# Decay attention with split operands: score operands stacked to 128 rows in batches 1 to 3

## The chip, the cores and the metric

The kernel runs on one core of one Trainium2 chip. The metric is the device time of one execution in microseconds (us); lower is better. TensorE (PE) multiplies, VectorE (DVE), ScalarE (ACT) and GpSimd (POOL) work on vectors, and SyncE's queue (SP) starts the transfers.

## What is computed

Attention with a decay and a causal mask (4 batches, 8 heads, 576 tokens, head width 64), then two dense layers. Cut to what matters:

```python
scores = scale * np.matmul(q, k.transpose(0, 1, 3, 2))
cum = np.cumsum(np.log(np.clip(f, 0.0001, 1.0)), axis=-1)
decay = cum[:, :, :, None] - cum[:, :, None, :]
scores = np.where(causal, -1e9, scores + decay)
scores = scores - np.max(scores, axis=-1, keepdims=True)
attn = np.exp(scores)
attn = attn / (np.sum(attn, axis=-1, keepdims=True) + 1e-09)
out = np.matmul(attn, v)
# then x = out as [2304, 512]
x = swish_1702(x @ w_in) @ w_out        # 512 -> 2048 -> 512
x = prelu(x @ w2_in, alpha) @ w2_out    # 512 -> 2048 -> 512
```

## The kernel before

**Order.** Nothing is issued where it is written. Each step is put into a plan (`plan.add`) with its costs on the engines that could do it, what it reads and writes, and a priority. `Plan.run` (L108) then places every step by these costs: it takes the step that can start first, attention before first-layer matmuls, and emits the instructions in that order. Each engine runs its own list in order. PE steps carry a mode: 0 for the full array, 1 for two 64-row halves, 2 for a split by columns; the planner counts 105 ns for a change of mode and avoids it for a while (L123 to L150). A tile belongs to a pool with a fixed number of slots, and a slot comes free when its last reader is done.

**Stages.** Attention works on a pair of heads at a time: batch 0 in two sweeps, then batches 1 to 3 with both chunks of a pair in turn, that is 12 pairs. Chunk 0 is queries 0 to 255, chunk 1 is queries 256 to 575. The first layer's matmuls (`gemm1`, L866) for blocks of 256 or 384 tokens are interleaved with the attention of later tokens and go on alone when it ends. Afterwards come the first layer's second half (L955), the second layer (L1045 and L1123) and the output. While batch 0 and the start of batch 1 run, DVE, ACT and POOL also turn the first layer's weights, which arrive as 64-bit numbers, into fp32 (L504 to L512).

**A pair of heads.** For precision an fp32 operand is split into a rounded part and the rest (KH and KL, QH and QL). Both heads share a tile: head 0 on partitions 0 to 63, head 1 on 64 to 127. In batches 1 to 3 `load_qk` (L531) fetches 32-row pieces, transposes them on DVE (L543), copies to the rounded part (L373 on ACT or L375 on DVE) and subtracts for the rest (L378 on DVE or POOL). DK holds the decay of the keys in two rows per head, and DQ the ones and the negated maxima of the queries.

- `chunk` finds the row maxima: QH times KH and ones times DK, each as one matmul per head on 64 rows, side by side (L669); the 64-row tail tile uses a zero-padded tile Z on the full array (L662, L663). DVE adds the mask and reduces (L678), POOL joins two halves of the tail (L687), PE turns the maxima (L695), and ACT or DVE writes them negated into DQ for both heads at once (L705, L707).
- `chunk2` computes the scores again, transposed, in four products (KH QH, KH QL, KL QH, DK DQ) for both heads side by side on 64 rows each (L794). ACT exponentiates into e (L801), POOL zeroes what is above the diagonal (L717).
- `after_scores` multiplies with the values. Chunk 0 uses fp32 products split by columns, 64 output columns per head part (L729, mode 2). Long tiles of chunk 1 are split into eh and el and multiplied on the full array (L758); the others go in fp32 (L735), the tail tile of 64 rows in mode 1. At last DVE transposes the sums (L815, L818), takes the reciprocal (L824), and multiplies (L835) into xr.

Pools that matter: KH, KL and DK have two slots, QH, QL and DQ three, e four.

Of the kernel before, what the change touches and what calls it, by code (L numbers as in the profile page):

```python
# [51 lines left out]
class Buf:  # L52
    def __init__(self, pool=None):
        self.pool = pool
        self.log = []
# [19 lines left out]
class Plan:  # L75
# [5 lines left out]
    def add(self, alts, fn, reads=(), writes=(), pri=0.0, lag=0.0, mode=0):  # L81
# [108 lines left out]
def kernel(  # L190
# [13 lines left out]
    nc = tc.nc  # L204
# [85 lines left out]
    p_z = sb("att", "Z", 2, [P, P], F32R)  # L290
# [16 lines left out]
    p_e = sb("att", "e", 4, [P, 2, 384])  # L307
# [5 lines left out]
    att_pools = [p_z, p_rk, p_rq, p_tk, p_tq, p_kh, p_kl, p_dk, p_qh, p_ql, p_dq, p_vr, p_vh, p_vl, p_mx, p_e, p_eh, p_el, p_tr, p_sm, p_rc]  # L313
# [68 lines left out]

    def a_out(n):
# [46 lines left out]
    for nm, p, view, n, val in (  # L430
        ("dk", p_dk, lambda x: (x.bitcast(F32), x[0:3].bitcast(F32), x[64:67].bitcast(F32)), 3 * S, (0.0, 1.0, 1.0)),
        ("z", p_z, lambda x: x.bitcast(F32), P, 0.0),
        ("dq", p_dq, lambda x: x.bitcast(F32), S - SPLIT, 0.0),
        ("mx", p_mx, lambda x: (x.bitcast(F32), x[:, 136:204].bitcast(F32), x[64:P, 138:139].bitcast(F32), x[0:64, 202:203].bitcast(F32)), 280, (-1.0, -0.5, 0.0, 0.0)),
        ("vr", p_vr, lambda x: x.rearrange("p t h c -> p t (h c)")[:, :, D:3 * D], NKT * P, 1.0),
# [10 lines left out]
    def filled(nm, p):  # L446
        return [fill[nm, len(p.bufs) - 1]] if len(p.bufs) <= p.n else []

# [82 lines left out]
    def load_qk(src, b, h0, c0, w, p_r, p_t, hi, lo, o0, pri, actq):  # L531

        raw, T = Buf(p_r), Buf(p_t)
# [10 lines left out]
        plan.add(a_copy(w), lambda e: copy(e, hi.ap[:, o0:o0 + w], T.ap[:, :w]), [T], [hi], pri)  # L544
        plan.add(a_sub(w), lambda e: sub(e, lo.ap[:, o0:o0 + w], T.ap[:, :w], hi.ap[:, o0:o0 + w].bitcast(F32)), [T, hi], [lo], pri)
# [24 lines left out]
    def prep_q(u, q0, q1, pri, actq, pet):  # L570
        b, h0, m = u["b"], 2 * u["hp"], q1 - q0
        qh, ql, dq = (Buf(x) for x in (p_qh, p_ql, p_dq))
        fdq = filled("dq", p_dq)
        if pet:
            load_pe(q, b, h0, q0, m, p_rq, qh, ql, 0, 0, pri)
        else:
            load_qk(q, b, h0, q0, m, p_rq, p_tq, qh, ql, 0, pri, actq)
        z = None
        if q0:
            z = Buf(p_z)  # L580
            fz = filled("z", p_z)
            for hh in range(2):
                plan.add(a_copy(64), lambda e, hh=hh: copy(
                    e, z.ap[64 * hh:64 * hh + 64, 64 * hh:64 * hh + 64], qh.ap[64 * hh:64 * hh + 64, m - 64:m].bitcast(F32)
                ), [qh, *fz], [(z, hh)], pri)
        return dict(u, z=z, fdq=fdq, qh=qh, ql=ql, dq=dq)

    def prep(b, hp, n, pri, early, actq, plain, pet):
        h0 = 2 * hp
        kh, kl, dk = (Buf(x) for x in (p_kh, p_kl, p_dk))  # L590
        fdk = filled("dk", p_dk)
        if pet:
            for i, (lo, hi) in enumerate(((0, SPLIT), (SPLIT, n))[:1 + (n > SPLIT)]):
# [581 lines left out]
```

## Time and profile before

| | us |
|---|---|
| three runs | 1023.01, 1023.96, 1024.02 |
| median | 1023.96 |
| profiled execution | 1022.32 |
| its span | 1020.6 |

The profile is of one execution. Times in it count from the start of the span. A row of the timeline gives a start, a length and an instruction; matmuls follow each other before the earlier has ended, so the distance from one start to the next says more than the length. In a matmul row `64*128 64x320` means 64 rows by 128 columns of fixed operand, and a moving operand of 64 rows by 320 columns; `x2` are two instructions merged.

### The profile page before, as it was taken

To read this page: it belongs to the slowest core of one execution; us is meant where nothing else is said; L and a number is where in the kernel's file an instruction comes from. 1 tells how busy PE (TensorE), PEld (TensorE's weight loads), DVE (VectorE), ACT (ScalarE), POOL (GpSimd) and SP (SyncE) were. 2 spreads that over 40 slices of the span, in tenths; PEclk is the share of its full clock that TensorE was granted. 3 is DMA by queue.
4 is the path that set the end of the run, shared out by engine and by line. 5 is a ranking of instruction groups with operands and counts; after the bars stand their busy time and mean duration, and the time that the engine had idled before them with its cause. 6 is when DMAs were issued, how large, how long until landed. Compare 5 with 4: busy or idle time off the path is not lost.

```text
span 1020.6 us, 17794 instructions
## 1 busy us (share of the span) xinstructions
PE 995.1 (98%) x6187; PEld 880.2 (86%) x6187; DVE 711.2 (70%) x1506; ACT 522.1 (51%) x1087; POOL 125.7 (12%) x209
## 2 busy tenths in 40 slices
PE   6799999999999999999999999999999999999997
PEld 4588789989888899988888988999999988888886
DVE  5688987767665493149996556567985866666773
ACT  4477755545444293258874554455774732222322
POOL 6124332323121100000000000000200110000000
PEclk9899999999999999999999999999999999999999
DMA  4597663443221176236765354655793534342451
GB/s 103 147 197 176 157 144 96 89 90 68 73 62 59 40 260 225 101 108 193 223 216 161 110 144 126 205 184 163 225 313 126 173 121 123 113 140 83 129 144 63
DMA packets 180089, 144.69 MB, mean 142 GB/s; under 512 B 101152, under 2 KB 155088, under 8 KB 180000
## 3 DMA queue, kind: packets, MB, share of 16 engines
q1 hardware_dynamic: 180000, 143.57, 48.3%
q8 instruction: 48, 0.79, 0.3%
q14 instruction: 41, 0.34, 0.1%
HBM read 96.14 MB, written 47.33 MB: 141 GB/s over the span
## 4 chain that ended last, share of the span: by engine, by line
PE 89%; DMA 4%; DVE 3%; issue 1%; ACT 1%; SPq 1%; POOL 0%; DVEq 0%; ACTq 0%; POOLq 0%
PE bk L866 20%; PE bk L955 19%; PE bk L1123 19%; PE bk L1045 13%; PE bk L794 5%; PE bk L758 3%; PE bk L669 2%; PE bk L735 2%; PE bk L729 2%; DMA rk<-in_k_dram 1%; DMA h2scr<-go 1%; DMA ba<-y1scr 1%; PE bk L695 1%; PE bk L564 1%; DMA wraw<-in_moe_w_out_dram 1%
## 5 line engine op out<-in xcount | busy, mean ns | idle before, releaser
L866 PE MATMUL bk<-xh,wA 128*128 128x384 f32 (+1 forms) x896 | 220.0, 319 | 1.5 <-POOL wA L378 1.3
L373 ACT CAST qh<-qg 128x512 fp32r<-128x512 f32 (+1 forms) x159 | 91.9, 579 | 170.8 <-DVE qg L921 117.0
L378 DVE TENSOR_TENSOR ql<-qg,qh 128x512 fp32r<-128x512 f32 (+1 forms) x158 | 100.7, 638 | 101.1 <-PE bk L955 50.6
L866 PEld LDWEIGHTS bk<-xh,wA 128*128 128x128 f32 x896 | 156.4, 189 | 12.3 <-issue 5.8
L1123 PE MATMUL bk<-wS,qh 128*128 128x512 f32 x576 | 145.7, 389 | 0.0
L866 PE MATMUL bk<-xl,wA 128*128 128x384 f32 (+1 forms) x448 | 140.0, 312 | 0.0
L1123 PEld LDWEIGHTS bk<-wS,qh 128*128 128x128 f32 x576 | 108.1, 188 | 22.4
L1045 PE MATMUL bk<-xsb,wS 128*128 128x384 f32 x576 | 108.1, 335 | 3.9 <-DVE go L1067 3.9
L678 DVE CUSTOM_DVE_ANT_0 bk<-bk,mask 128x512 f32<-128x512 f32 (+4 forms) x160 | 75.4, 494 | 45.0 <-PE bk L669 28.9
L1045 PEld LDWEIGHTS bk<-xsb,wS 128*128 128x128 f32 x576 | 100.3, 188 | 5.5 <-DVE go L1067 5.2
L955 PE MATMUL bk<-qh,woa 128*128 128x512 f32 (+1 forms) x440 | 99.5, 368 | 0.0
L373 ACT COPY gg<-bk 128x384 f32<-128x384 f32 (+1 forms) x109 | 47.4, 435 | 93.8 <-PE bk L866 86.0
L955 PEld LDWEIGHTS bk<-qh,woa 128*128 128x128 f32 x440 | 77.3, 189 | 14.0 <-ACT qh L373 0.4
L866 PEld LDWEIGHTS bk<-xl,wA 128*128 128x128 f32 x448 | 84.6, 189 | 0.1
L1045 PE MATMUL bk<-xsa,wS 128*128 128x384 f32 x432 | 82.6, 335 | 0.0
L801 ACT ACTIVATE e<-bk 128x384 f32<-128x384 f32 (+3 forms) x192 | 60.3, 396 | 40.7 <-PE bk L794 40.6
L1123 PE MATMUL bk<-wS,ql 128*128 128x512 f32 x288 | 80.4, 389 | 0.0
L1045 PEld LDWEIGHTS bk<-xsa,wS 128*128 128x128 f32 x432 | 75.6, 188 | 0.4 <-DVE xsa L378 0.3
L914 DVE SCALAR_TENSOR_TENSOR qg<-qg,qr 128x512 f32<-128x512 f32 (+1 forms) x80 | 50.8, 636 | 23.6 <-ACT qg L913 23.2
L1123 PEld LDWEIGHTS bk<-wS,ql 128*128 128x128 f32 x288 | 54.1, 188 | 11.2
L913 ACT ACTIVATE qg<-qr 128x512 f32<-128x512 f32 (+1 forms) x80 | 47.0, 588 | 22.5 <-DVE ql L378 20.9
L955 PE MATMUL bk<-ql,woa 128*128 128x512 f32 (+1 forms) x220 | 54.1, 368 | 0.0
(163 smaller groups left out, 1775.7 us busy)
## 6 DMA issues: line engine op xcount, KB each, us to landing
h2scr<-go SPq DMA_DIRECT2D x96, 192.0 KB
wraw<-in_moe_w_in_dram SPq DMA_DIRECT2D x32, 512.0 KB
wraw<-in_moe_w_out_dram SPq DMA_DIRECT2D x32, 512.0 KB
qr<-h1scr SPq DMA_DIRECT2D x64, 256.0 KB
qr<-h2scr SPq DMA_DIRECT2D x64, 256.0 KB
h1scr<-gg SPq DMA_DIRECT2D x64, 192.0 KB
ba<-y1scr SPq DMA_DIRECT2D x24, 384.0 KB
h1scr<-gg SPq DMA_DIRECT2D x48, 128.0 KB
```

What stands on the lines that cost most here:

```text
L373: nc.scalar.copy(dst, src)
L378: E[e].tensor_tensor(dst, a, b, op=ALU.subtract)
L678: plan.add([("DVE", c_dve(c1 - c0) + 90.0)], lambda e, pm=pm, c0=c0, c1=c1, mk=mk, m0=m0, col=col, f0=f0: nc.vector.tensor_tensor_reduce(p ...
L758: nc.tensor.matmul(pb[hh].ap[:l.shape[1], s0 - q0:n], l, rhs.ap[:w, hh, :m], start=st, stop=sp, skip_group_check=True,)
L794: nc.tensor.matmul(pss[hh].ap[:w, o_:o_ + m], x.ap[r, a:a + w], y.ap[r, s0 - q0:n], start=i == 0, stop=i == 3, skip_group_check=True)
L801: plan.add([("ACT", c_act(x1 - x0, True))], lambda e, hh=hh, pss=pss, e32=e32, w=w, x0=x0, x1=x1: nc.scalar.activation(e32.ap[:w, hh, :x1 ...
L866: nc.tensor.matmul(ph.ap[:, :n], w.ap[:, a, c, :], x[c // 2].ap[:, c % 2, :n], start=(c == 0 and j == 0), stop=(c == KT - 1 and j == 2))
L913: plan.add([("ACT", c_act(n))], lambda e: nc.scalar.activation(g.ap[:, :n], raw.ap[:, :n], AF.Tanh, scale=0.851), [raw], [g], pri)
L914: plan.add([("DVE", c_dve(n), 0.0, True)], lambda e: nc.vector.scalar_tensor_tensor(g.ap[:, :n], g.ap[:, :n], 1.0, raw.ap[:, :n], op0=ALU. ...
L955: nc.tensor.matmul(py[d].ap[:, :n], w[:, a, d * P:(d + 1) * P], (lo if x else h).ap[:, :n], start=(k == 0 and (a, x) == (0, 0)), stop=(k = ...
L1045: nc.tensor.matmul(out.ap[:, :XH], w[:, a, t, c, :], x.ap[:, b, c, :], start=(st and c == 0 and i == 0), stop=(c == 1 and i == 2), skip_gr ...
L1123: nc.tensor.matmul(py[t].ap, (lo if x else h).ap[:, t * P:(t + 1) * P], w[:, a], start=(k == 0 and (a, x) == (0, 0)), stop=(k == NM - 1 an ...
```

## The change

In batches 1 to 3 each head gets a plane of its own with 128 rows. KA holds a head's rounded keys in 64 rows, and beside them the decay rows; KB holds the rest of the keys in 64 rows and the rounded keys in the other 64. QA and QB are laid out to match: against KB stands the rounded query beside the rest, so that one product over 128 rows gives KL QH and KH QL together, and KA QA gives KH QH and the decay term (66 rows for the maxima and 67 for the scores of head 0, 128 of head 1). So a score tile has two products per head instead of four, and a maxima tile one instead of two, all in mode 0. To fill the planes, `load_qk` copies and subtracts by half (one half for each head) and moves the rounded halves across with a second copy (`a_move`, on ACT, DVE or POOL). The ones and zeros are set by POOL memsets at a slot's first use (`refill`), and one row of QA for each chunk. The negated maxima are evicted head by head. Chunk 0 of these batches takes the full-width fp32 value product (L735) and the by-head normalisation that chunk 1 has. The fp32 product of the 64-row tail tile takes 128 rows with zeros in all batches. The separate tq tile goes, tk serves both, the query planes have two slots, and e three. Batch 0 keeps its products in views of the new tiles.

The diff, cut to its core:

```diff
...
-    p_tq = sb("att", "tq", 1, [P, S - SPLIT])
-
-    p_kh = sb("att", "KH", 2, [P, S], F32R)
-    p_kl = sb("att", "KL", 2, [P, S], F32R)
-    p_dk = sb("att", "DK", 2, [P, S], F32R)
-    p_qh = sb("att", "QH", 3, [P, S - SPLIT], F32R)
-    p_ql = sb("att", "QL", 3, [P, S - SPLIT], F32R)
-    p_dq = sb("att", "DQ", 3, [P, S - SPLIT], F32R)
+
+    p_ka = sb("att", "KA", 2, [P, 2, S], F32R)
+    p_kb = sb("att", "KB", 2, [P, 2, S], F32R)
+    p_qa = sb("att", "QA", 2, [P, 2, S - SPLIT], F32R)
+    p_qb = sb("att", "QB", 2, [P, 2, S - SPLIT], F32R)
...
-    p_e = sb("att", "e", 4, [P, 2, 384])
+    p_e = sb("att", "e", 3, [P, 2, 384])
...
+    def a_move(n):
+        return [*a_copy(n), ("POOL", c_pool(n), 0.0, True)]
...
+        ("vr", p_vr, lambda x: (x.rearrange("p t h c -> p t (h c)")[:, :, D:3 * D], x[64:P, NKT - 1]), NKT * P + 2 * P, (1.0, 0.0)),
+        ("e", p_e, lambda x: x[64:P, :, 0:64], P, 0.0),
...
+    def refill(buf, first, n, sets, pri):
+
+        if len(buf.pool.bufs) - first <= buf.pool.n:
+            plan.add([("POOL", 0.95 * n + 120.0)], lambda e: [E[e].memset(x.bitcast(F32), y) for x, y in sets(buf.ap)], (), [buf], pri)
...
+    def load_qk(src, b, h0, w, c0, p_r, big, other, keys, swap, pri, actq):
...
+        raw, T = Buf(p_r), Buf(p_tk)
...
-        plan.add(a_copy(w), lambda e: copy(e, hi.ap[:, o0:o0 + w], T.ap[:, :w]), [T], [hi], pri)
-        plan.add(a_sub(w), lambda e: sub(e, lo.ap[:, o0:o0 + w], T.ap[:, :w], hi.ap[:, o0:o0 + w].bitcast(F32)), [T, hi], [lo], pri)
+        half = [slice(64 * hh, 64 * hh + 64) for hh in range(2)]
+        for hh, r in enumerate(half):
+            plan.add(a_copy(w), lambda e, hh=hh, r=r: copy(e, big.ap[r, hh, :w], T.ap[r, :w]), [T], [(big, ("h", hh, k_)) for k_ in keys], pri)
+        for hh, r in enumerate(half):
+            x, y = (half[1 - hh], r) if swap else (r, half[1 - hh])
+            rb = [(big, ("h", hh, k_)) for k_ in keys]
+            plan.add(a_sub(w), lambda e, hh=hh, r=r, y=y: sub(
+                e, other.ap[y, hh, :w], T.ap[r, :w], big.ap[r, hh, :w].bitcast(F32)
+            ), [T, *rb], [(other, ("l", hh, k_)) for k_ in keys], pri)
+            plan.add(a_move(w), lambda e, hh=hh, r=r, x=x: copy(e, other.ap[x, hh, :w], big.ap[r, hh, :w].bitcast(F32)), rb, [(other, ("h", hh, k_)) for k_ in keys], pri)
...
+        if not pet:
+            refill(qa, 2 * NP, 3 * m, lambda x: ((x[64:67, 0], 1.0), (x[0:64, 1], 0.0), (x[0:3, 1], 1.0)), pri - 1)
+            plan.add([("POOL", 0.95 * m + 60.0)], lambda e: E[e].memset(qa.ap[0:1, 1, :m].bitcast(F32), 0.0), (), [(qa, ("d", 1))], pri)
...
+            refill(ka, 2 * NP, 3 * S, lambda x: ((x[64:67, 0], 1.0), (x[0:64, 1], 0.0), (x[0:3, 1], 1.0)), pri - 1)
+            load_qk(k, b, h0, n, 0, p_rk, ka, kb, range(len(ends)), False, pri, actq)
+            for hh, r0 in enumerate((64, 1)):
+                plan.add(DMA(8 * n), lambda e, hh=hh, r0=r0: nc.sync.dma_start(
+                    ka.ap[r0:r0 + 2, hh, :n].bitcast(F32), cscr[:, r + hh, :n]
+                ), [*((b_cum, (p_, i)) for p_ in range(len(ends)) for i in range(2))], [(ka, ("d", hh))], pri)
...
+                    if not old:
+                        for hh in range(2):
+                            r = slice(0, 66 if hh == 0 else P)
+                            if w < P:
+                                nc.tensor.matmul(pms[0].ap[:, :c1 - c0], z.ap[r, hh], ka.ap[r, hh, c0:c1], start=hh == 0, stop=hh == 1)
+                            else:
+                                nc.tensor.matmul(pms[hh].ap[:, f0:f0 + c1 - c0], qa.ap[r, hh, a - q0:a - q0 + w], ka.ap[r, hh, c0:c1], start=True, stop=True, skip_group_check=True)
+                        return
...
+                plan.add([("PE", 2 * c_mm(c1 - c0, P))], mm, rd, [(x, f0) for x in pms], pri, mode=1 if w == P and old else 0)
...
+            for hh, r in enumerate((slice(64, 67), slice(0, 3))):
+                plan.add([("ACT", c_act(n, True)), ("DVE", c_dve(n))], lambda e, hh=hh, r=r: ev(e, qa.ap[r, hh, :n], pt.ap[r, :n]), [pt], [(qa, ("d", hh))], pri)
...
-        n, both = q1 - q0, q0 == 0
+        n, both = q1 - q0, q0 == 0 and u["plain"]
...
-                            pb[hh].ap[:, c0:c1], vr.ap[:w, t, hh, :], e32.ap[:w, hh, e0:e0 + m],
+                            pb[hh].ap[:, c0:c1], vr.ap[:, t, hh, :], e32.ap[:, hh, e0:e0 + m],
...
-            plan.add([("PE", cost)], av32, [vr, e32, *u["fvr"]], pb, pri, mode=2 if both else 1 if w < P else 0)
+            plan.add([("PE", cost)], av32, [vr, e32, *u["fvr"]], pb, pri, mode=2 if both else 0)
...
+                if not old:
+                    for hh in range(2):
+                        for i, (x, y, r) in enumerate(((kb, qb, slice(0, P)), (ka, qa, slice(0, 67 if hh == 0 else P)))):
+                            nc.tensor.matmul(pss[hh].ap[:w, o_:o_ + m], x.ap[r, hh, a:a + w], y.ap[r, hh, s0 - q0:n], start=i == 0, stop=i == 1, skip_group_check=True)
+                    return
...
+            plan.add([("PE", 4 * c_mm(m, w))], sc, rd, [(x, o_) for x in pss], pri, mode=1 if old else 0)
...
+        both = both and old
...
```

## Rows read from the trace of the kernel before

**Rows 1.** Chain of waits in time order, after the attention: start us, us, what.

```profile
356.34 18.75 PE bk L866 x108
```

**Rows 2.** Busy table, one period: stretch, length, busy us (instructions), PEclk, DMA, GB/s.

```profile
207.19:226.45 19.26, 19.26 (x185) 17.36 (x187) 14.26 (x44) 9.69 (x26) 5.39 (x10) 1.00 0.37 81
```

**Rows 3.** The same table where batch 1 begins.

```profile
107.00:131.00 24.00, 20.98 (x194) 17.72 (x194) 23.39 (x66) 17.08 (x41) 10.92 (x18) 1.00 0.61 155
```

**Rows 4.** PE timeline, full array to 64-row halves: start us, us, engine, line, operation.

```profile
209.65 0.28 PE L866 MATMUL bk<-xl,wA 128*128 128x256 f32 x1
209.77 0.28 PE L866 MATMUL bk<-xh,wA 128*128 128x256 f32 x1
...
209.98 0.33 PE L669 MATMUL bk<-KH,QH 64*128 64x128 f32 x2
210.15 0.28 PE L669 MATMUL bk<-DK,ones 64*128 64x128 f32 x2
210.26 0.30 PE L794 MATMUL bk<-QH,KH 64*128 64x192 f32 x2
...
211.31 0.31 PE L794 MATMUL bk<-QH,KL 64*128 64x320 f32 x2
211.46 0.31 PE L794 MATMUL bk<-DQ,DK 64*128 64x320 f32 x2
211.70 0.66 PE L729 MATMUL bk<-e,VR 128*64 128x128 f32 x8
212.29 0.38 PE L669 MATMUL bk<-KH,QH 64*128 64x256 f32 x2
212.51 0.28 PE L669 MATMUL bk<-DK,ones 64*128 64x256 f32 x2
```

**Rows 5.** PE timeline, 64-row halves back to the full array.

```profile
213.64 0.31 PE L794 MATMUL bk<-DQ,DK 64*128 64x320 f32 x2
213.88 0.39 PE L866 MATMUL bk<-xh,wA 128*128 128x256 f32 x1
214.10 0.28 PE L866 MATMUL bk<-xl,wA 128*128 128x256 f32 x1
```

**Rows 6.** PE timeline around a column-split value product (L729).

```profile
206.91 0.28 PE L866 MATMUL bk<-xh,wA 128*128 128x256 f32 x1
207.12 1.08 PE L729 MATMUL bk<-e,VR 128*64 128x256 f32 x8
208.13 0.39 PE L866 MATMUL bk<-xh,wA 128*128 128x256 f32 x1
208.35 0.28 PE L866 MATMUL bk<-xl,wA 128*128 128x256 f32 x1
```

**Rows 7.** PE timeline around a full-width fp32 value product (L735).

```profile
196.32 0.81 PE L735 MATMUL bk<-e,VR 128*128 128x192 f32 x4
196.84 0.59 PE L758 MATMUL bk<-eh,VH 128*128 128x320 f32 x2
197.27 0.46 PE L758 MATMUL bk<-eh,VL 128*64 128x320 f32 x2
197.56 0.46 PE L758 MATMUL bk<-el,VH 128*128 128x320 f32 x2
```

**Rows 8.** Groups by form in that period: busy us, mean ns, idle before.

```profile
L373 ACT CAST KH<-tk 128x576 fp32r<-128x576 f32 x1 | 0.7, 678 | 0.0
...
L835 DVE TENSOR_TENSOR xr<-bk,tr 64x320 f32<-64x320 f32 x3 | 1.4, 481 | 0.0
L378 DVE TENSOR_TENSOR KL<-tk,KH 128x576 fp32r<-128x576 f32 x1 | 0.8, 759 | 0.0
...
L378 POOL TENSOR_TENSOR QL<-tq,QH 128x320 fp32r<-128x320 f32 x1 | 0.9, 874 | 2.0 <-DVE QH L375 2.0
```

**Rows 9.** DVE and POOL timelines about 91 us.

```profile
91.15 1.17 DVE L506 TENSOR_SCALAR wc<-wc 128x512 int32<-128x512 int32 x1 [0.57 <-ACT wc L504]
...
90.72 1.31 POOL L512 TENSOR_TENSOR wc<-wc,wraw 128x512 int32<-128x512 int32 x1 [1.62 <-issue]
```

More of the change, by code (lines that the diff above doesn't have):

```diff
@@ L65, in ap @@
     def ap(self):
+        if self.parent is not None:
+            return self.parent.ap[:, self.i]
         if self.slot not in self.pool.tiles:
@@ L99, in add @@
                     buf.left += 1
+                if buf.parent is not None and buf.parent not in op.bufs:
+                    op.bufs.append(buf.parent)
+                    buf.parent.left += 1
         deps.discard(op)
@@ L639, in chunk @@
     def chunk(u, q0, q1, pri):
-        kh, dk, qh, dq, z = u["kh"], u["dk"], u["qh"], u["dq"], u["z"]
+        old, ka, qa, z = u["plain"], u["ka"], u["qa"], u["z"]
+        if old:
+            kh, dk, qh, dq = u["kh"], u["dk"], u["qh"], u["dq"]
         dkp = lambda c: [(dk, (i, p_)) for i in range(2) for p_ in range(2 if c > SPLIT else 1)]
         kp = lambda x, c: [(x, p_) for p_ in range(2 if c > SPLIT else 1)]
+        kn = lambda c: [(ka, ("h", hh, p_)) for hh in range(2) for p_ in range(2 if c > SPLIT else 1)] + [(ka, ("d", 0)), (ka, ("d", 1))]
         mx = Buf(p_mx)
         fmx = filled("mx", p_mx)
+        if not old:
+            refill(mx, 2 * NP, 280, lambda x: ((x, -1.0), (x[:, 136:204], -0.5), (x[0:64, 136:137], 0.0), (x[64:P, 202:203], 0.0)), pri - 1)
         n = q1 - q0
@@ L707, in ev @@
                 nc.vector.tensor_scalar_mul(d, s_, -1.0)
-        plan.add([("ACT", c_act(n, True)), ("DVE", c_dve(n))], ev, [pt, *u["fdq"]], [dq], pri)
+        if old:
+            plan.add([("ACT", c_act(n, True)), ("DVE", c_dve(n))], ev, [pt, *u["fdq"]], [dq], pri)
+        else:
+            for hh, r in enumerate((slice(64, 67), slice(0, 3))):
+                plan.add([("ACT", c_act(n, True)), ("DVE", c_dve(n))], lambda e, hh=hh, r=r: ev(e, qa.ap[r, hh, :n], pt.ap[r, :n]), [pt], [(qa, ("d", hh))], pri)
         return dict(u=u, q0=q0, q1=q1, pri=pri)
@@ L784, in chunk2 @@
                 e32, e0 = Buf(p_e), 0
+                fe = filled("e", p_e)
             else:
@@ L790, in sc @@
             def sc(e, pss=pss, a=a, w=w, s0=s0, m=m, o_=o_):
+                if not old:
+                    for hh in range(2):
+                        for i, (x, y, r) in enumerate(((kb, qb, slice(0, P)), (ka, qa, slice(0, 67 if hh == 0 else P)))):
+                            nc.tensor.matmul(pss[hh].ap[:w, o_:o_ + m], x.ap[r, hh, a:a + w], y.ap[r, hh, s0 - q0:n], start=i == 0, stop=i == 1, skip_group_check=True)
+                    return
                 for i, (x, y) in enumerate(((kh, qh), (kh, ql), (kl, qh), (dk, dq))):
@@ L802, in chunk2 @@
                     e32.ap[:w, hh, :x1 - x0], pss[hh].ap[:w, x0:x1], AF.Exp, scale=0.125
-                ), [pss[hh] if both else (pss[hh], o_)], [(e32, hh)], pri)
+                ), [pss[hh] if both else (pss[hh], o_), *fe], [(e32, hh)], pri)
             if both and i_ == 0:
```

95 lines of the change are left out of this document (55 added, 40 removed).

## The prediction

> **What bounds the kernel now.** I read four views in this order. First the chain of waits: when the attention ends at 356 us it runs on through first-layer matmuls (L866) back to back, the first stretch 18.75 us long [rows 1]. These belong to tokens whose attention was done long before: there was always a stock of such work. Then the busy table, cut into periods of one pair of heads (one batch, two heads, both chunks) in batches 1 to 3: in a steady period of 19.26 us TensorE (PE) is busy all 19.26, VectorE (DVE) 14.26, ScalarE (ACT) 9.69 and GpSimd (POOL) 5.39 [rows 2]. The granted clock there is 1.00 (2.4 GHz), so it has nothing to give back. PE is never idle because L866 fills every hole; so in this stage a PE nanosecond taken out shortens the kernel, and a longer vector chain is hidden until it outruns PE. Third, PE's timeline: a busy PE is not a PE at peak, so I look at the distance from one start to the next. Fourth, the busy table again at 107 to 131 us, where batch 1 begins: there PE does only 20.98 of 24 us and DVE 23.39 of 24 [rows 3]. That short stage is bound by DVE, which also prepares the first layer's weights.
>
> **Where PE loses time.** Inside one kind of work the starts are regular: 0.12 us for a full-array L866 of 256 columns, 0.11 for a side-by-side pair of 64-row L669 of 128 columns, about 0.15 for a pair of L794 of 320 [rows 4]. They break where the kind changes:
> - full array to 64-row halves: the last L866 starts at 209.77, so L669 should start at 209.89; it starts at 209.98, and its next comes after 0.17 instead of 0.11 [rows 4]. Loss 0.09 + 0.06 = 0.15 us.
> - back to the full array: the last L794 pair at 213.64 would let L866 start at 213.79; it starts at 213.88 and its next comes after 0.22 instead of 0.12 [rows 5]. Loss 0.09 + 0.10 = 0.19 us.
> - the column-split value product L729, 256 columns: from 207.03 (206.91 + 0.12) to 208.23 (208.35 - 0.12) it takes 1.20 us with both borders [rows 6]. The 128-column one, from 211.61 to 212.39 (212.51 - 0.12): 0.78 us [rows 4].
>
> **The change, part by part, on PE.** Per pair the two chunks keep their column passes. A score tile was four products, each run for both heads side by side in two 64-row halves: four slots. Now it is two 128-row products for each of two heads: four slots. Maxima were two slots and stay two. Of 320 columns a 64-row pair takes 0.15 (L794 at 211.31) and a 128-row matmul 0.145 (two L758 in 0.29) [rows 4, 7], so I price a slot alike. No row shows a contraction of 66 or 67 rows, which the decay rows of the first head now have; nearest are these 64- and 128-row ones, equal in time, so I take no difference (below zero is excluded, since the columns streamed are the same; above is a rival). The tail tile's value product goes from 64 to 128 rows with the same four instructions of 64 columns: nothing; the end above is one more border in the four pairs of batch 0, 4 x 0.34 = 1.4 us, of which I take 0.5.
> What goes:
> - two visits to the 64-row kind, each with a border in and out: 2 x (0.15 + 0.19) = 0.68 us.
> - L729 becomes the same full-width product as L735. Of that, 192 columns run from 196.32 to 196.98 (197.27 less the 0.29 that two L758 need), 0.66 us, with no gap at either side [rows 7]. By columns 256 cost 0.88 and 128 cost 0.44, so 1.20 - 0.88 = 0.32 and 0.78 - 0.44 = 0.34 are saved.
> Sum 1.34 us a pair, 12 pairs: **16 us**. With each border at its dearest reading (0.20) it is 12 x (0.80 + 0.70) = 18. I take 16.5.
>
> **What is added on the other engines.** Each load of keys or queries is now written in halves: two copies, two subtractions and two further copies instead of one copy and one subtraction. A half has 64 partitions but all its columns, and a 64-partition operation isn't half price: L835 takes 0.48 for 64x320, and KL's subtraction 0.76 for 128x576, that is 0.42 for 320 columns [rows 8]. Per pair the queries (256 + 320 columns) are as long as the keys (576), so every step counts twice 576 columns:
> - one more copy: 2 x 0.68 = 1.4 us on ACT; one more subtraction: 2 x 0.76 = 1.5 on DVE, or on POOL about 2 x 1.6 (0.87 for 320) [rows 8]; two moves: 4 x 0.68 = 2.7 on ACT.
> - the negated maxima are evicted twice for each chunk: two more of 256 and 320 columns, by KH's length 0.7 on ACT.
> - chunk 0 is normalised by head: one more transpose and one more multiply of 64x256, by L835 0.4 each, 0.8 on DVE.
> ACT gets 4.8 more, 14.5 in all; DVE 2.3 more, 16.6; against a new period of 19.26 - 1.34 = 17.9 us. That is 81% and 93%. It fits, with PE work of earlier tokens as the cover; if that cover fails PE waits for what is over 17.9.
> - Waits added: L669 now waits for a POOL memset of one row per chunk, and behind it on PE stand all L866. POOL has 13.9 us idle in a period [rows 2], so nothing; the end above is one POOL operation (0.87), twice a pair. QA has two slots where QH had three: a chunk's copies wait until the scores two chunks before are done. In the period shown those end at 213.8 and PE goes on with L866 [rows 5], under which two half copies (0.3 to 0.4 each) fit; the end above is those 0.8 us, once a chunk. In batch 0 the key tiles, with the same lifetime, had two slots already, so nothing. Three e tiles instead of four delay a fourth exp by one value product; the cover is again L866.
> - The one-off memsets in POOL (about a dozen, at most 0.87 each) fall about where batch 1 begins, where POOL is busy 10.92 of 24 us [rows 3]: nothing on PE.
> - DMAs: as many per pair on SP's queue as before; the two decay rows go by head rather than by part. Nothing moves past another queue.
> - In the DVE-bound stretch of 24 us (1.25 pairs) the gain of 1.7 us is lost, since DVE sets the pace, and up to 1.25 x 2.3 = 2.9 come on top; I take 1.3, as POOL can take the subtractions. Loss 3.0.
> Sum against the profiled execution of 1022.3 us (span 1020.6): -16.5 + 0.5 + 3.0 = -13, so 1009.3. The median of the runs is 1.6 above that execution: **1010.5**.
>
> **Rivals.**
> *DVE becomes the bound (slower).* If the four moves go to DVE too, at up to KL's 0.76 each [rows 8], it needs 16.6 + 3.0 = 19.6 us a pair, and POOL operations hold it up besides: an L506 that started at 91.15 ended only at 92.32, 0.29 after the POOL operation of 90.72 to 92.03, so 0.88 of it was a block [rows 9]. One such block a pair makes 20.5. From 17.9 each microsecond eats gain, from 19.26 the kernel is slower: 12 x (20.5 - 19.26) = +15, so 1039; without the block +4, so 1028. For it: DVE at 93% on paper. Against: 5.0 us of DVE idle now, and ACT with room for the moves [rows 2]. The Trainium skill, SBUF — State Buffer, "Who interferes with whom", says that a GpSimd operation that reads SBUF and a two-input VectorE operation shut each other out for their whole length, and so does VectorE in its two-port modes. The L506 row agrees; were it true of every pair of operations, DVE and POOL would be one engine with 14.26 + 5.39 = 19.65 us of work in a period of 19.26, and the added work would go straight onto the path; the trace shows that it holds for some of them only.
> *Only the column split matters.* If the breaks at 64-row work come from something else that stays (the first weight load after a wait), only L729's 0.66 a pair goes: -8 + 3.5, 1019.5. Against: 128-row L758 next to L735 has no break [rows 7].
> *The odd rows count as another kind.* If a 66- or 67-row matmul next to a 128-row one paid a border, some 26 a pair at 0.17 would cost 12 x 4.4 = 53: 1060. Nothing in the trace speaks for it but the absence of a row.
>
> **How the numbers follow.** Forecast 0.65 (1003 to 1016: the lower end is 18 us of gain, none of the losses, and the 3.0 us that PE idles at 107 to 131 us filled by a new order); the partial gain 0.13 (1016 to 1021.5); DVE so near the bound that gain and loss cancel 0.06; DVE the bound 0.13; odd rows 0.03. About 0.2% (2 us) is what a measurement of this kernel can tell from no change. So faster 0.78, same 0.06, slower 0.16. The range 1003 to 1025 takes in the first three cases; the rest, 0.16, is left out.
>
> **What would show it.** Right: no 64-row matmuls after batch 0, L866 starts 0.12 behind an attention matmul, a steady period near 17.9 us, the attention over some 13 us earlier and the later stages unchanged. Wrong: PE idle in the steady periods with DVE or ACT as releaser, DVE at 99%, a gap before the 67-row matmuls, or PE idle at 107 to 131 us far above the 3.0 of now.

## The result: 1% slower, and where the time went

| us | before | after |
|---|---|---|
| median (4 runs each) | 1023.49 (1021.50 to 1024.02) | 1033.29 (1032.45 to 1034.24) |
| profiled execution, its span | 1022.32, 1020.6 | 1032.45, 1030.7 |

The ratio is 1.010, with a 95% interval of 1.0082 to 1.0117. The forecast was 1010.5, so it missed by 22.8 us and on the wrong side.

First the head of the page of after: busy time, share of the span, instructions of each engine. TensorE has 528 matmuls fewer than before (6187), as the products per tile say it should, and its busy time is 43 us short of the span.

```profile
span 1030.7 us, 17052 instructions
PE 987.5 (96%) x5659; PEld 886.3 (86%) x5659; DVE 765.9 (74%) x1596; ACT 573.7 (56%) x1188; POOL 140.2 (14%) x266
```

Next the busy table of after: stretch, length, then busy us (instructions) of PE, PEld, DVE, ACT, POOL, then granted clock, DMA share and GB/s. The first row answers to [rows 3]; the second is a stretch of six pairs and answers to [rows 2].

```profile
107.00:131.00 24.00, 18.18 (x106) 14.83 (x103) 22.19 (x51) 17.05 (x43) 10.03 (x20) 0.86 0.45 103
198.04:333.98 135.94, 131.05 (x894) 125.54 (x892) 115.52 (x303) 92.29 (x226) 33.36 (x69) 1.00 0.34 82
...
50.00:100.00 50.00, 47.36 (x359) 39.68 (x358) 39.47 (x90) 35.34 (x86) 18.51 (x33) 0.96 0.82 196
100.00:150.00 50.00, 40.50 (x278) 35.21 (x277) 47.41 (x113) 37.43 (x88) 23.15 (x43) 0.93 0.47 115
150.00:200.00 50.00, 47.00 (x352) 44.13 (x351) 46.34 (x130) 32.71 (x82) 14.18 (x29) 1.00 0.40 96
```

PE is idle 2.6 us from 50 to 100, 9.5 from 100 to 150 and 3.0 from 150 to 200. The kernel before, in the same view, idles 0.2, 3.2 and 0 (the last row is four steady pairs):

```profile
50.00:100.00 50.00, 49.79 (x392) 41.95 (x391) 42.60 (x109) 35.65 (x95) 17.33 (x25) 0.98 0.85 187
100.00:125.00 25.00, 23.31 (x211) 19.95 (x210) 24.52 (x66) 20.21 (x48) 8.06 (x13) 1.00 0.64 165
125.00:150.00 25.00, 23.47 (x211) 20.94 (x209) 24.29 (x69) 14.07 (x38) 10.06 (x15) 1.00 0.56 126
150.00:200.00 50.00, 50.00 (x481) 44.81 (x481) 36.09 (x106) 27.74 (x73) 15.88 (x25) 1.00 0.41 97
...
170.43:247.46 77.03, 77.03 (x734) 69.46 (x733) 57.09 (x170) 39.91 (x106) 21.59 (x36) 1.00 0.38 83
```

In the six steady pairs of after PE idles 4.9 us, 0.8 a pair, where it had idled nothing. A pair now takes some 22.7 us instead of 19.26, with more first-layer matmuls between its steps, and the attention's last value product starts at 377.2 us instead of 355.9. The second half of the first layer ends at 648.7 us against 639.2, so 9.5 of the 10.1 us of span are lost up to there.

**The borders are gone, as forecast.** PE's timeline of after (start, us, engine, line, operation):

```profile
263.04 0.34 PE L942 MATMUL bk<-xh,wA 128*128 128x384 f32 x1
263.22 0.31 PE L859 MATMUL bk<-QB,KB 128*128 128x320 f32 x1
263.36 0.31 PE L859 MATMUL bk<-QA,KA 67*128 67x320 f32 x1
263.51 0.31 PE L859 MATMUL bk<-QB,KB 128*128 128x320 f32 x1
263.66 0.30 PE L859 MATMUL bk<-QA,KA 128*128 128x320 f32 x1
263.80 0.34 PE L942 MATMUL bk<-xh,wA 128*128 128x384 f32 x1
```

From a first-layer matmul to the scores and back no start comes late: 0.18, then 0.14 to 0.15 four times, with 67 rows as with 128. The 0.15 and 0.19 us at the borders of [rows 4, 5] are not there. The value product by full width is free of them too:

```profile
212.05 0.28 PE L942 MATMUL bk<-xh,wA 128*128 128x256 f32 x1
212.17 1.03 PE L796 MATMUL bk<-e,VR 128*128 128x256 f32 x4
212.85 0.47 PE L942 MATMUL bk<-xh,wA 128*128 128x256 f32 x1
213.15 0.28 PE L942 MATMUL bk<-xl,wA 128*128 128x256 f32 x1
```

Read as [rows 6] were, the 256 columns take from 212.17 to 213.03 (213.15 less the 0.12 of an L942), 0.86 us, where the split product took 1.20 with its borders. The row at 212.85 starts early and is no end of the product, since its own successor comes 0.30 later.

**What took their place.** The waits of PE in after (who waits for whom: us in total, times, longest):

```profile
PE bk L859 <- ACT QA L762: 3.0, 1, 3.0
...
PE bk L796 <- POOL e L778: 2.6, 3, 1.3
PE bk L819 <- ACT eh L377: 2.3, 3, 0.9
PE bk L942 <- DVE xl L382: 2.1, 3, 1.5
PE bk L751 <- DVE MX L734: 1.8, 4, 0.6
PE bk L710 <- POOL QA L599: 1.6, 1, 1.6
PE bk L942 <- POOL wA L382: 1.5, 2, 0.8
```

Many waits, each short, on three engines; no single one carries the loss. Two of the longest, 3.0 and 1.6, stand next to each other, where batch 1 begins. Timelines of the engines there, in brackets the idle time before and what ended it:

```profile
111.69 0.45 PE L710 MATMUL bk<-KA,QA 128*128 128x384 f32 x1 [1.63 <-POOL QA L599]
115.26 0.48 PE L859 MATMUL bk<-QA,KA 67*128 67x128 f32 x1 [3.04 <-ACT QA L762]
...
108.11 1.19 POOL L460 MEMSET QA<- 3x320 f32 x3 [1.02 <-PE bk L864]
109.33 1.99 POOL L460 MEMSET KA<- 3x576 f32 x3
111.28 0.35 POOL L599 MEMSET QA<- 1x320 f32 x1
...
112.22 1.27 POOL L525 TENSOR_TENSOR wc<-wc,wraw 128x512 int32<-128x512 int32 x1
...
111.31 3.05 DVE L382 TENSOR_TENSOR QB<-tk,QA 64x320 fp32r<-64x320 f32 x2
114.39 0.41 DVE L764 TENSOR_SCALAR QA<-bk 3x256 fp32r<-3x256 f32 x1
...
114.84 0.37 ACT L762 ACTIVATE QA<-bk 3x256 fp32r<-3x256 f32 x1 [3.41 <-DVE QA L764]
...
109.00:116.00 7.00, 2.33 (x11) 1.63 (x11) 6.91 (x13) 3.46 (x11) 4.34 (x8) 0.72 0.35 95
112.00:119.00 7.00, 3.96 (x13) 3.19 (x12) 6.81 (x12) 4.03 (x8) 1.90 (x3) 0.51 0.50 117
```

Read it from the top of POOL's part. The first-use memset of a query slot waits for PE's last batch-0 scores (L864), whose queries were in it (there are two slots now); a memset of a key slot, whose keys are copied only at 115.76, goes ahead of the row memset (L599) for which the maxima (L710) wait. DVE's two rests of queries take 3.05 us (2.53 and 0.49), though twelve like them take 0.51 each in the steady pairs. Behind them on DVE is L764, behind that on ACT L762, and behind that the scores: PE worked 2.33 of 7 us. The granted clock, the last column but two, falls in the same stretch: from 105 to 112 us it is still 1.00, with PE busy for 5.30 of 7 us, and from 112 to 119 it is 0.51, which at levels of 2.4 and 1.2 GHz is 6.9 us at 1.2 GHz. PE is busy for 3.96 us there, at half the pace, so the clock costs about 2 us on top of the wait. The kernel before has 1.00 in this stretch [rows 3].

**A ledger.** I added up PE's time over its slots: the time from the first start in a stretch to the first start behind it, less a slot for each matmul. The slot is the planner's own price: n/2.4 + 13.5 ns for n columns, so 147 for 320, where the rows above show 140 to 150, and at least 111 from 128 columns on and 57 below. Two matmuls side by side share one; an instruction of the fp32 value product is taken at twice n/2.4, as the rows at 212 show (its 64 columns at 98, the turned maxima at 62 and 30). Idle time, borders and the lower clock are all in it. From 0 to 650 us the differences between kernels agree with those of the profiled spans to 3 us, so a stretch is good to about 2. The table is of the profiled executions, whose times stand beside the medians.

| us over the slots | median | profiled | 50–100 | 100–150 | 150–200 | 200–350 |
|---|---|---|---|---|---|---|
| before | 1023.5 | 1022.3 | 6.6 | 8.8 | 4.5 | 13.7 |
| after | 1033.3 | 1032.5 | 9.8 | 15.5 | 6.5 | 10.8 |
| e_head0 | 1020.5 | 1024.0 | 10.9 | 13.7 | 5.6 | 3.3 |
| e_nomove | 1031.9 | 1030.6 | 10.5 | 9.9 | 10.3 | 7.8 |
| e_costs | 1030.8 | 1030.4 | 11.1 | 14.3 | 8.4 | 5.0 |
| e_late | 1031.6 | 1030.2 | 9.7 | 10.3 | 10.9 | 10.2 |
| l12_120 | 1023.1 | 1022.3 | 10.0 | 8.4 | 12.7 | 2.7 |
| e_halves | 1032.7 | 1030.4 | 8.7 | 14.4 | 4.4 | 13.7 |
| e_q2 | 1029.3 | 1027.8 | 10.8 | 9.2 | 5.1 | 13.3 |
| b_costs | 1027.4 | 1027.3 | 8.8 | 10.6 | 3.9 | 13.1 |

Before, PE does not idle from 200 to 350, and the 13.7 are borders and small irregularities. Kernels that have neither borders nor idle time there keep 2.7 and 3.3 (l12_120, e_head0), so the borders are 10.4 to 11.0, that is 1.3 to 1.4 us for each of the 7.8 periods of 19.26. In after the borders are gone and waits fill most of their place: 10.8. From 50 to 100 us after has 3.2 more than before, although batch 0, which runs until 108 us, keeps its products of queries and keys.

### The profile page after: what moved, and what is told of

The parts are those of the page before. It is cut to its first block, busy times and chain, and to the rows that moved or that the text cites. A ratio compares the mean times of both kernels' runs of the same rounds, so it can differ in the third digit from the quotient of the medians.

```text
span 1030.7 us, 17052 instructions
## 1 busy us (share of the span) xinstructions
PE 987.5 (96%) x5659; PEld 886.3 (86%) x5659; DVE 765.9 (74%) x1596; ACT 573.7 (56%) x1188; POOL 140.2 (14%) x266
## 4 chain that ended last, share of the span: by engine, by line
PE 76%; DVE 7%; ACT 3%; DMA 3%; issue 2%; POOL 1%; SPq 0%; DVEq 0%; ACTq 0%; POOLq 0%
PE bk L1031 19%; PE bk L1199 19%; PE bk L942 15%; PE bk L1121 13%; PE bk L796 3%; PE bk L859 3%; PE bk L819 2%; DVE bk L734 1%; DMA h2scr<-go 1%; PE bk L710 1%; PE bk L864 1%; ACT e L876 1%; DMA wraw<-in_moe_w_out_dram 1%; DVE tr L894 1%; DVE QB L382 1%
## 5 line engine op out<-in xcount | busy, mean ns | idle before, releaser
L942 PE MATMUL bk<-xh,wA 128*128 128x384 f32 (+1 forms) x896 | 221.3, 317 | 4.0 <-POOL wA L382 1.5
L942 PEld LDWEIGHTS bk<-xh,wA 128*128 128x128 f32 x896 | 157.1, 189 | 7.9 <-POOL wA L382 2.1
L942 PE MATMUL bk<-xl,wA 128*128 128x384 f32 (+1 forms) x448 | 140.6, 314 | 2.2 <-DVE xl L382 2.1
L1031 PEld LDWEIGHTS bk<-qh,woa 128*128 128x128 f32 x440 | 77.4, 189 | 13.7
L734 DVE CUSTOM_DVE_ANT_0 bk<-bk,mask 128x512 f32<-128x512 f32 (+4 forms) x160 | 74.8, 490 | 17.9 <-PE bk L721 9.5
L942 PEld LDWEIGHTS bk<-xl,wA 128*128 128x128 f32 x448 | 84.6, 189 | 3.9 <-DVE xl L382 3.3
L876 ACT ACTIVATE e<-bk 128x384 f32<-128x384 f32 (+3 forms) x192 | 62.5, 395 | 26.3 <-PE bk L859 14.6
L1199 PEld LDWEIGHTS bk<-wS,ql 128*128 128x128 f32 x288 | 54.1, 188 | 11.1
L796 PE MATMUL bk<-e,VR 128*128 128x192 f32 (+4 forms) x272 | 57.1, 339 | 2.8 <-POOL e L778 2.6
```

The lines of the kernel that those rows point to most:

```text
L734: plan.add([("DVE", c_dve(c1 - c0) + 90.0)], lambda e, pm=pm, c0=c0, c1=c1, mk=mk, m0=m0, col=col, f0=f0: nc.vector.tensor_tensor_reduce(p ...
L796: nc.tensor.matmul(pb[hh].ap[:, c0:c1], vr.ap[:, t, hh, :], e32.ap[:, hh, e0:e0 + m], start=st, stop=sp, skip_group_check=True,)
L876: plan.add([("ACT", c_act(x1 - x0, True))], lambda e, hh=hh, pss=pss, e32=e32, w=w, x0=x0, x1=x1: nc.scalar.activation(e32.ap[:w, hh, :x1 ...
L942: nc.tensor.matmul(ph.ap[:, :n], w.ap[:, a, c, :], x[c // 2].ap[:, c % 2, :n], start=(c == 0 and j == 0), stop=(c == KT - 1 and j == 2))
L1031: nc.tensor.matmul(py[d].ap[:, :n], w[:, a, d * P:(d + 1) * P], (lo if x else h).ap[:, :n], start=(k == 0 and (a, x) == (0, 0)), stop=(k = ...
L1199: nc.tensor.matmul(py[t].ap, (lo if x else h).ap[:, t * P:(t + 1) * P], w[:, a], start=(k == 0 and (a, x) == (0, 0)), stop=(k == NM - 1 an ...
```

## The experiments

Theory after the result: the border saving is real, and is spent because the added vector work is late, above all where batch 1 begins; the rivals are the fewer slots, the memsets, and the mere fact that the planner now emits another order. Each kernel was timed beside the kernel before on the same chip (1023.0 to 1024.3).

**One part of the change in the kernel before.** The column split of chunk 0:

```diff
-        n, both = q1 - q0, q0 == 0
+        n, both = q1 - q0, q0 == 0 and u["plain"]
```

(and the normalisation by head in the same batches.)

> The kernel before with one part of the change alone: chunk 0 of batches 1 to 3 takes the full-width value product and the normalisation by head; everything else stays. Theory (PE is bound and the borders cost what was read: 0.66 us a pair for L729, 12 pairs, DVE 0.8 us a pair under cover): 7 to 8 us faster, about 1016. Rival (the borders are worth little, the gain on PE was misread): within 1 us of the kernel before.

1026.4 us, ratio 1.0036 (1.0006 to 1.0067), with six runs from 1021.7 to 1031.0: no more above before than the controls below, and no gain, where 7 to 8 us were expected. The profile is of the fastest run. From 150 to 350 us it has 14.8 over the slots instead of 18.2, some 0.3 us a pair, which is half of what was read for L729; from 50 to 150 us it has 3.5 more. So a part of the split's border saving comes without the stacked scores, and this order spends it elsewhere. Why only half of it shows is open.

Fewer slots, together and one by one:

```diff
-    p_qh = sb("att", "QH", 3, ...)      # e_slots, e_q2; the same for QL and DQ
+    p_qh = sb("att", "QH", 2, ...)
-    p_e = sb("att", "e", 4, ...)        # e_slots, e_e3
+    p_e = sb("att", "e", 3, ...)
```

> The kernel before with QH, QL and DQ cut from three slots to two and e from four to three, as in the change, and nothing else. Theory (fewer slots cost at the start, where PE idled 17.0 us instead of 13.2 before 100 us, and where batch 1 begins): 3 to 5 us slower, with the added idle before 130 us. Rival (the key tiles had two slots anyway, so the slots are harmless): within 1 us.

> The kernel before with QH, QL and DQ at two slots instead of three, e left at four. With both cut the kernel was 0.6% slower. Theory (a chunk's query copies must wait for the scores two chunks back): 3 to 6 us slower than before, nearly all of it. Rival (it was e): within 1 us of before.

> The kernel before with e at three slots instead of four, the query tiles left at three. Theory (the query slots cost, not e): within 1.5 us of before. Rival (the fourth exponential waits for a value product while there is no first-layer work to fill with): 3 to 6 us slower.

1030.19 together (1.0061, 1.0039 to 1.0082), 1029.28 with two query slots (1.0061, 1.0040 to 1.0081), 1026.66 with three e tiles (1.0016, 1.0005 to 1.0027). Another order alone costs some 3.4 (the controls below), so of the 5 to 6 us something like 2 may be the slots themselves. The loss stands in batch 0: from 50 to 100 us PE idles 7.6 us with both cut and 3.7 with two query slots, against 0.2 before and 1.9 and 1.2 in the two controls.

The load of queries and keys by halves, with no other gain or cost:

```diff
-        plan.add(a_copy(w), ... copy(e, hi.ap[:, o0:o0 + w], T.ap[:, :w]) ...)
+        for hh, r in enumerate(half):     # the subtraction likewise
+            plan.add(a_copy(w), ... copy(e, hi.ap[r, o0:o0 + w], T.ap[r, :w]) ...)
```

> The kernel before, but in batches 1 to 3 each copy and each subtraction of load_qk is done as two operations of 64 partitions (as in the change, without moves and without new tiles): per pair about 1.4 us more on ACT and 1.5 on DVE or POOL. Theory (vector work is not hidden here, PE waits for it): 4 to 8 us slower. Rival (hidden under the stock of first-layer matmuls): within 1.5 us of before.

1032.72 (1.0076, 1.0053 to 1.0099): the added copy and subtraction alone cost the kernel before 8.5 us, about 5 above the controls. Most of it stands where batch 1 begins: from 100 to 150 us it is 14.4 over the slots instead of 8.8 (the two controls have 10.6 and 9.5), and from 200 to 350 it is 13.7 as before. So added vector work is not hidden at that start, and it is hidden in the steady pairs.

**One part undone in the kernel after.** Without the moves of rounded halves:

```diff
-  plan.add(a_move(w), ... copy(e, other.ap[x, hh, :w], big.ap[r, hh, :w]) ...)
+  refill(other, 2 * NP, w, lambda y, x=x, hh=hh: ((y[x, hh], 0.0),), pri - 1)
```

> The changed kernel without the second copy of each half (the rounded keys and queries in KB and QB are left at zero, so the small correction products are left out of the scores of batches 1 to 3); PE's instructions stay. Theory (the added vector work makes PE wait 7.7 us between 150 and 350 us): that idle falls to 3 or less and the kernel comes to 1026 to 1028. Rival (vector work is hidden, only the start of batch 1 costs): the idle stays and the time is within 1.5 us of 1033.

1031.92, 1.4 below after, which is hardly more than the spread of the runs; 1026 to 1028 was expected. Without the moves (six a pair, nearly all on ACT) 9.9 instead of 15.5 us are lost from 100 to 150 and 7.8 instead of 10.8 after 200, but 10.3 instead of 6.5 from 150 to 200. Its zero fills put POOL at 20.15 of 25 us from 100 to 125, so the 1.4 are a lower bound of what the moves cost.

Only the first head prepared; the second head's rows and the moved rows stay zero:

```diff
+            if hh == 0:
                 plan.add(a_copy(w), ... big.ap[r, hh, :w] ...)
-        for hh, r in enumerate(half):
+        refill(other, 2 * NP, 2 * w, lambda y: ((y, 0.0),), pri - 1)
+        for hh, r in enumerate(half[:1]):
...
-            plan.add(a_move(w), ...)
```

> The changed kernel with only the first head of each pair prepared in batches 1 to 3 (its copy and its rest; the second head's copies and rests and all the moves of rounded halves are left out, their rows stay zero, so the values are not the reference's). TensorE runs every instruction of the changed kernel, and VectorE and ScalarE prepare no more operations per pair than before. If the added vector work is what ate the saving, the idle TensorE time from 100 to 200 us falls from 12 us to under 4 and the kernel comes to 1010 to 1018 us, that is 15 to 23 below the changed kernel. If the fewer slots, the refills or the changed order of the program did it, the time stays within 5 us of the changed kernel (1027 or more).

1020.45 (0.9968, 0.9949 to 0.9987): faster than before, 12.8 below after. Its profile is of the slowest of ten runs (1024.02). The busy table (columns as above):

```profile
100.00:125.00 25.00, 20.45 (x125) 17.20 (x124) 20.57 (x48) 14.65 (x36) 19.01 (x36) 0.82 0.56 153
...
198.00:334.00 136.00, 135.94 (x955) 133.35 (x954) 113.07 (x320) 74.07 (x187) 34.64 (x75) 1.00 0.35 84
```

In the steady stretch PE idles 0.06 instead of 4.9 us, and from 200 to 350 us the time over the slots falls from 10.8 to 3.3: there the waits come from the second head's vector work. But it is not the 1010 to 1018 that the theory gave. Where batch 1 begins little is gained in this execution: 13.7 instead of 15.5 over the slots from 100 to 150, and from 100 to 125 us PE still idles 4.6 with a granted clock of 0.82 and POOL at 19.0 of 25. POOL fills more there than in after (this kernel's own zeros), and the slots and the second eviction are as in after; I can't divide that part further.

**Controls: the same instructions in another order.** The planner places every step by its own costs. The controls scale its three cost functions of DVE, ACT and POOL in batches 1 to 3 and change nothing else:

```diff
-        return n / (1.92 if fast else 0.96) + 68.0
+        return SC[0] * (n / (1.92 if fast else 0.96) + 68.0)     # and ACT and POOL likewise
...
+        SC[0] = 1.12 if no >= 8 else 1.0                         # 0.97, 1.06, 1.2, 1.25 in others
```

> The kernel before, with the planner's costs of VectorE, ScalarE and GpSimd work 12% higher in batches 1 to 3: the same instructions in another static order. A control: if another order by itself moves the time, this kernel differs from before by 3 to 8 us with no instruction added; if order is worth nothing, it stays within 2 us (1022 to 1026).

> The same control the other way: the planner's costs of VectorE, ScalarE and GpSimd work 3% lower in batches 1 to 3. Order worth nothing: 1022 to 1026 us. Order worth as much as the single edits tried before (fewer query slots +5, fewer exponential slots +2.4): 1026 to 1031 us.

1027.4 (1.0033, 1.0018 to 1.0048) and 1027.5 (1.0031, 1.0018 to 1.0043). The kernel before loses some 3.4 us by another order alone, whichever way the costs go. In its steady part, 200 to 350 us, PE idles 0.0 and 0.7 us; from 50 to 150 us the time over the slots is 19.4 and 17.5 instead of 15.4, and the rest is spread in steps of about 1 us.

> The changed kernel with the planner's vector costs 3% lower in batches 1 to 3: nearly the order that it has. If its loss is vector work on the path, any order near its own loses as much: 1030 to 1037 us. If 1033 is an unlucky order, as another order alone moved the kernel before by 4, this one may fall to 1028 or less.

> The changed kernel with the planner's costs of ACT, DVE and POOL operations multiplied by 1.12 for batches 1 to 3; the same operations in another order. Theory (the order is planned for vector operations shorter than they are, so PE runs into them): less PE idle between 150 and 350 us, 3 to 6 us faster than the changed kernel. Rival (the vector engines simply have too much to do): the idle moves but does not fall, within 2 us of 1033 or slower.

> The changed kernel with the planner's vector costs 25% higher in batches 1 to 3, twice as much as the 12% that gave 1030.8. If late vector work that the order did not allow for is what costs after 200 us, the wait there goes to nearly none and the time is 1027 to 1031; if the vector work itself is the bound at the start of batch 1, the loss there stays and the time is 1030 to 1034.

The kernel after: 1031.87 with 3% less (1.0073, 1.0054 to 1.0093), 1030.76 with 12% more (1.0068, 1.0046 to 1.0090), 1036.71 with 25% more (1.0129, 1.0108 to 1.0150). So 1033 is no unlucky order. With 12% the wait after 200 us goes (5.0 over the slots instead of 10.8), but the start of batch 1 stays at 14.3; with 25%, for which 1027 to 1034 was expected, the start grows to 24.6.

**Where the change pays.** Batch 1 in the old form on the new tiles, the change from batch 2 on:

```diff
-        if not pet:
+        if not u["old"]:            # old: pairs before NEW = 12 (10, 14 in others); 8 is batch 1's first
...
+            load_old(q, b, h0, q0, m, p_rq, p_tk, qh, ql, 0, pri, actq)
```

> The changed kernel, but batch 1 is still done the old way (64-row halves, with the new tiles and their fewer slots); batches 2 and 3 take the change, so that the first use of the new planes falls where the first layer's weights are long done. Theory (the loss is made where batch 1 begins: between 100 and 150 us PE lost 18 us to waits, 9 before): 1024 to 1027, with 9 to 11 us lost there. Rival (the added vector work of every pair costs, wherever it is): 4 of 12 pairs without it, 1029 to 1031. Third (the first use of the planes costs the same wherever it falls): 1032 to 1034.

> The same with the planner's vector costs 6% higher. A real recovery: between the 1031.6 at 0% and the 1024.7 at 12%, 1025 to 1029 us. One lucky order: 1029 to 1033.

> Batch 1 in the old form (with the new tiles and their fewer slots), batches 2 and 3 changed, and the planner's vector costs 12% higher in batches 1 to 3. If the changed kernel lost by late vector work that the order did not allow for, the two mends add up: 1026 to 1029 us, against 1031.6 for the first alone and 1030.8 for the second. If each only moves the same wait elsewhere, 1030 to 1033 us.

> Batch 1 in the old form, batches 2 and 3 changed, planner's vector costs 20% higher (12% gave 1024.7). A real recovery: 1022 to 1027 us, with under 7 us above the instruction times from 200 to 400 us (before 16). One lucky order: 1029 to 1033.

1031.6 (1.0073, 1.0050 to 1.0095) with the planner's own costs, where the theory had 1024 to 1027: the start of batch 1 is nearly as before (10.3 over the slots from 100 to 150 us), but 10.9 are lost from 150 to 200, where the form changes, and the waits after 200 stay (10.2). 1024.36 (1.0009, 0.9994 to 1.0024), 1024.73 (1.0014, 0.9990 to 1.0037) and 1023.13 (0.9995, 0.9976 to 1.0014) with vector costs 6, 12 and 20% higher. Three neighbours agree, so it is no single lucky order. Either mend alone gives about 2 us against after, both give 8.6 to 10.2, and the loss against before is gone; a gain is not there. From 200 to 350 us PE idles 3.7 us with the planner's own costs, and 1.3, 0.6 and 0.0 with costs 6, 12 and 20% higher. Busy table of l12_120, then POOL where its change of form falls:

```profile
175.00:200.00 25.00, 20.46 (x187) 15.92 (x186) 23.13 (x66) 15.21 (x41) 16.16 (x43) 1.00 0.21 38
...
200.00:350.00 150.00, 150.00 (x1028) 147.86 (x1027) 125.51 (x338) 96.46 (x229) 45.09 (x83) 1.00 0.35 86
...
177.93 2.06 POOL L464 MEMSET KA<- 3x576 f32 x3
179.95 0.93 POOL L464 MEMSET Z<- 128x256 f32 x4
```

From 200 to 350 us PE is busy all 150, with every added operation done, and the ledger shows a gain of 11.0 there. It is spent at the switch (8.2 more than before from 150 to 200), where PE idles 4.5 of 25 us while the memsets run and DVE has 23.1 of 25, and in batch 0 (3.4 more from 50 to 100).

> The change from the third pair of batch 1 on (the first two pairs in the old form), planner's vector costs 6% higher. If the loss sits where VectorE is full, from 100 to 150 us, it comes back here: 1027 to 1033 us. If the loss is only the switch from one form to the other, wherever it stands, the time stays near the 1024.4 of the change from batch 2 on.

> The change from the third pair of batch 2 on, planner's vector costs 6% higher. If the changed form is worth about 1 us a pair where it is covered, two pairs less make it 1 to 3 us slower than the 1024.4 of the change from batch 2 on: 1025 to 1028 us. If the switch is cheaper this late than the two pairs bring, 1021 to 1024.

From the third pair of batch 1 on: 1027.37 (1.0058, 1.0042 to 1.0075), with 10.1 over the slots from 100 to 150 us and 10.5 from 150 to 200 (l12_106: 10.6 and 6.2). From the third pair of batch 2 on: 1025.83 (1.0034, 1.0020 to 1.0047). Earlier is worse by 3.0, and the loss stands at this kernel's own switch rather than before 150 us, where the expectation had it; later is worse by 1.5 with two pairs less, which fits about 0.7 us a pair but is hardly more than the intervals.

## Why the prediction was wrong

**Borders and column split, 16.5 us: right in mechanism and size.** No 64-row matmul remains after batch 0, the spacing is regular, and 66 and 67 rows cost as 128. Where PE does not wait (l12_120, 200 to 350 us) the time over the slots is 2.7 instead of 13.7; 11.0 over the 7.8 old periods is 1.4 us a pair, against 1.34 in the sum. The Trainium skill, TensorEngine Tiling (Array Packing), "Key Properties", says that a change of the tiling mode drains TensorE; the breaks of before and their absence in after agree, and it gives no price. The rivals that only the split matters and that odd rows are another kind are refuted.

**"It fits, with PE work of earlier tokens as the cover": this step failed.** The second head's vector work is worth 12.8 us in all (e_head0), where I had it at nothing beyond the 3.0. The condition of the step was named, and the profile before showed that it does not hold where batch 1 begins: [rows 3] has PE idle for 3.0 of 24 us, 1.3 of them in one wait for first-layer weights (wA), so there was little stock of that work. I charged that stretch 3.0 us as a loss of pace. It came to 6.7 more than before over the slots from 100 to 150 us (15.5 against 8.8) and 2.0 more up to 200, and some 2 of it are the clock, which no term had. That added vector work alone does this is shown in the kernel before (e_halves, 5.6 more from 100 to 150 us); how much of it in after is vector work and how much the memsets and slots, the runs don't divide, since e_head0 keeps most of the loss there and e_nomove sheds most of it. The stretch is also longer than 24 us: DVE has 46.3 of 50 us from 150 to 200 (before 36.1).

**In the steady pairs the load did fit, the order did not.** The period that I expected to fall to 17.9 us rose to 22.7, and the attention ended 21 us later instead of 13 earlier. That by itself costs nothing, since first-layer matmuls fill the time: in l12_120 the attention ends as late (379.4) with PE busy throughout. DVE went from 57.09/4 = 14.3 (four pairs of before) to 115.52/6 = 19.3 us a pair, ACT from 10.0 to 15.4; I had added 2.3 and 4.8. What I had priced on DVE, the rests of the load and chunk 0's normalisation, came to 2.5. The other 2.5 are operations that the plan now gives to DVE: 1.0 a pair for rests of e (el, 8 in four pairs before, with 4 more on POOL, and 19 in six pairs now), the rest for copies, for rests of x and for maxima. Groups of DVE, and one of ACT, in those pairs (line, operation, count, busy us, mean ns, idle before), the first of before, the others of after:

```profile
L378 DVE TENSOR_TENSOR el<-e,eh 128x640 fp32r<-128x640 f32 x8 | 6.6, 821 | 0.0
...
L382 DVE TENSOR_TENSOR el<-e,eh 128x640 fp32r<-128x640 f32 x19 | 16.0, 856 | 4.6 <-ACT eh L377 4.4
L377 ACT CAST eh<-e 128x640 fp32r<-128x640 f32 x13 | 9.4, 734 | 0.6 <-POOL e L778 0.5
...
L764 DVE TENSOR_SCALAR QA<-bk 3x320 fp32r<-3x320 f32 x5 | 2.4, 479 | 3.9 <-ACT QA L762 3.8
...
L764 DVE TENSOR_SCALAR QA<-bk 3x256 fp32r<-3x256 f32 x5 | 2.1, 417 | 0.5 <-ACT QA L762 0.4
...
L382 DVE TENSOR_TENSOR KB<-tk,KA 64x576 fp32r<-64x576 f32 x11 | 8.4, 765 | 1.1 <-ACT KA L377 0.9
L382 DVE TENSOR_TENSOR QB<-tk,QA 64x320 fp32r<-64x320 f32 x12 | 6.1, 508 | 0.2
```

Still DVE is busy for 85% and not at its bound, so the rival "DVE becomes the bound" has the right sign and a time in its range (1028 to 1039), but not its mechanism. The 4.9 us of PE's idle time there come from the order: the plan counts 401 ns for a rest of 320 columns (320/0.96 + 68) and it takes 508, 668 for one of 576 that takes 765, and 626 for the copy of e to eh on ACT that takes 734. For this copy (L819 behind ACT's eh) PE waits longest, 2.3 of the 4.9 us. A step placed a little early on PE's list holds up everything behind it. l12_120 does the same work with DVE at 84% and no idle PE, and the idle time shrinks step by step as the plan counts more (3.7, 1.3, 0.6, 0.0). I had read cover as a matter of busy shares.

**Slots and memsets, "nothing".** The chain at 108 to 115 us shows a price: the query slot freed late and a memset that nobody needed yet ahead of one that PE waited for, 1.63 us of PE. The two query slots cost the kernel before 5.1 us, of which some 2 are above the controls. "In batch 0 ... nothing" failed too: after loses 3.2 us there from 50 to 100, and every kernel in the table with its slots 3 to 5; the controls, with the old slots, lose 2.2 and 1.4, so slots and order both have a part. That tk now serves queries too I had not priced at all; in the six pairs no wait shows ahead of its transposes, and no run isolates it.

**What the sum could not hold.** Another order alone costs the kernel before some 3.4 us in both controls. An edit that makes the planner place the work anew can cost as much before anything else, and [rows 2] can't show it. If this and the 12.8 for the second head simply add, 22.8 - 12.8 - 3.4, some 6 to 7 us, are left for slots, memsets and the rest; no run shows that they add, and since each run is an order of its own, each of these shares is good to about 3 us. A slip stands in the forecast as well: 1009.3 + 1.6 is 1010.9, not 1010.5, which changes nothing.

## What to carry to other kernels

A saving on the busiest engine counts only while there is other work to fill the waits of what feeds it: look for the stretch where the stock is empty (here the start of batch 1) and price the added work there, with its waits and the lower clock that can come with them, not by mean busy shares. Where a program places its work by a cost table, run a control that moves the order and nothing else before giving a few microseconds to a cause, and bring the table up to the measured durations before judging a change that loads those engines.

## What the runs showed of the hardware

- Partitions were no part of a vector operation's price here: on DVE a subtraction of 576 columns took 759 ns on 128 partitions before [rows 8] and 765 on 64 in after, and evicting maxima of 256 columns took 414 ns on 67 partitions before (L707) and 417 on 3 (L764).
- A rest of 64x320 on DVE (two inputs) took 2.53 us at 111.31, with POOL's L599, L778 and L525 running from 111.28 to 113.49; the next one, with POOL done, took 0.49, and the mean of twelve others is 0.51. The Trainium skill, SBUF — State Buffer, "Who interferes with whom", has a two-input VectorE operation and a GpSimd operation that reads SBUF shut each other out; L778 and L525 read SBUF and this row agrees. The mean of 508 ns shows that such a block is rare in the steady pairs.
- From 112 to 119 us of after the granted clock was 0.51, 1.2 GHz nearly throughout. PE had been busy for 5.30 of the 7 us before, at full clock, and then stood for 3.0 us. The kernel before, busy for 20.98 of the 24 us from 107 on, kept full clock [rows 3].
